# Pooled-query attention and a softplus feed-forward layer: the plan's model of DMAs, its tables, and which pairs' sums TensorE takes

## The chip, the cores and the metric

The kernel runs on one core of a Trainium2 chip. The metric is the device time of one execution in microseconds.

## The reference

```
q_pool = q.reshape(B, H, S // 2, 2, D).mean(axis=3)          # B 4, H 8, S 1152, D 64
scores = scale * np.matmul(q_pool, k.transpose(0, 1, 3, 2))
scores = scores - np.max(scores, axis=-1, keepdims=True)
attn = np.exp(scores)
attn = attn / (np.sum(attn, axis=-1, keepdims=True) + 1e-09)
attn_out = np.matmul(attn, v)
x = attn_out.transpose(0, 2, 1, 3).reshape(B * 576, 512)
h = x @ w_in                                                  # 512 -> 2048
g = np.maximum(h, 0.0) + np.log1p(np.exp(-np.abs(h)))         # softplus
out = g @ w_out                                               # 2048 -> 512
```

Queries are pooled by twos, so there are 576 of them for 1152 keys in each of 32 heads. The two weight matrices arrive as 8-byte floats.

## The kernel before

Two heads make a pair, and there are 16 pairs, numbered 0 to 15; four pairs are a batch. Queries, keys, weights and activations are split into a high and a low f16 part, so that products of f16 keep more digits.

For a pair, `prepare` loads keys, queries and values on SyncE's queue, sums the two queries of a pool (VectorE or GpSimd), finds a scale from squares (ScalarE, a small matmul, a few tiny VectorE steps), writes the high halves (`hi_ways`: ScalarE, GpSimd or VectorE) and the low halves (`lo_ways`: VectorE or GpSimd) and turns keys and queries by DMA transposes (`kT<-kcat`, `qA<-qcat`). `maxima` then computes all scores once, in 27 matmul groups of 384 columns, and VectorE reduces each of them to a negative maximum (`nm<-m`); the maxima become two more columns of the low queries (`qlow<-nm`, the shift steps).

`attention` computes the scores again, turned, in 18 steps for a pair: nine tiles of 128 keys for 256 queries of both heads (512 columns) and nine for 320 (640 columns). In each step TensorE makes the scores (`s`), ScalarE the exponentials (`p`), TensorE the products with the values (`pv`). The sums of the exponentials come in one of two ways. For pairs in `SUMMED` TensorE adds a block of small matmuls with ones to every step (line 871). For the others VectorE or GpSimd adds the tiles `p` elementwise into `acc` (16 adds for a pair), and a closing block of the same size (line 932) sums over the partitions. At the end of a half the sums go out of `rinv` by a small DMA to `few`, get inverted there, go to DRAM (`scratch`) and come back spread over partitions; VectorE or GpSimd multiplies them onto the outputs `xT`.

`feed_forward` takes eight blocks of 256 or 384 rows: matmuls up, softplus on ScalarE, a split into `gh` and `gl`, matmuls down, a store. `weights` decodes `w_in` in eight blocks (1024 KB each, loaded into `gh` and `gl`) and `w_out` in sixteen, mostly on VectorE. `ORDER` interleaves pairs (u) and blocks (U up, D down): pairs 0 to 4 stand alone, then blocks and pairs alternate, and three blocks stand alone at the end.

No order on an engine is written out by hand. Every operation is a `Task` with a priority, the ways (engines) in which it can run, their assumed durations, and the buffers that it takes and gives back. `Sched.run` plays a model of the five queues in time: whenever an engine is free, the ready task with the lowest priority number that fits its buffers is taken, unless another engine would finish it sooner, and is emitted there. So tables and assumed durations decide both the engine and the order. `NUDGE` adds a number to the priority by kind of task and pair or block. VectorE and GpSimd tasks marked "port" are kept apart in that model. On the chip each queue runs in order, and semaphores hold an instruction until what it reads is there.

DMAs all go out on SyncE. Before the change a DMA occupied the model's queue for bytes / 350 + 100 ns (or a fixed number), and its result was `late` by another fixed number.

Of the kernel before, what the change touches and what calls it, by code (L numbers as in the profile page):

```python
# [33 lines left out]
    "up": [-26.25, -7.25, 5.25, -1, 8, -13, -11.5, 6.25],
    "down": [0, -2, 3, -1.75, 12.75, -22.75, -0.25, 7.5],
# [16 lines left out]
class Task:  # L52
    __slots__ = ("ways", "deps", "after", "prio", "take", "give", "ready", "begun", "price", "late")

    def __init__(self, ways, prio, take, give):
        self.ways, self.prio, self.take, self.give = ways, prio, take, give
        self.begun, self.price, self.late = False, {}, 0.0
        self.deps, self.after, self.ready = 0, [], {w[0]: 0.0 for w in ways}


class Sched:
# [9 lines left out]
        "DMA": {"DVE": 100.0, "ACT": 100.0, "POOL": 100.0, "PE": 100.0, "DMA": 1400.0},  # L71
# [22 lines left out]
    def run(self):  # L94
        free = {}
        cold = self.COLD
        port, table = 0.0, "exp"
# [26 lines left out]
        while events:  # L124
# [97 lines left out]
def tile_attention_softplus_ffn(  # L222
# [179 lines left out]
    def load(fn, nbytes, deps, prio, take):  # L402
        return task([("DMA", dma(nbytes), fn)], deps, prio, take=take, late=2600.0)
# [8 lines left out]
    SUMMED = range(5)  # L412
# [84 lines left out]
    def w_in(g, prio):  # L497
# [7 lines left out]
            1 << 19 << (W64 - 1), last_on[g % 2], prio, [])  # L505
# [32 lines left out]
    def w_out(f, prio):  # L538
# [6 lines left out]
        def words(e):  # L545
# [3 lines left out]
                  1 << 18 << (W64 - 1), [], prio, [r])  # L549
# [42 lines left out]
    def prepare(u):  # L592
# [14 lines left out]
        def low():  # L607
# [12 lines left out]
            2 * S * D * 4, [], prio - 6.0, [r])  # L620
# [26 lines left out]
        ql = load(load_q, 1000000, [], prio - 6.0, [qr])  # L647
# [9 lines left out]
        for h in range(2):  # L657
# [496 lines left out]
```

## Time and profile before

| | |
|---|---|
| three runs, us | 863.42, 863.89, 864.05 |
| profiled execution, us | 864.61 |
| its span, us | 862.5 |
| TensorE busy, us (share) | 815.5 (95%) |
| VectorE | 608.2 (71%) |
| ScalarE | 424.1 (49%) |
| GpSimd | 197.9 (23%) |
| granted TensorE clock | 0.998 of 2.4 GHz |

The span is the time from the first to the last instruction in the profiled execution. Busy time is the time in which an engine has an instruction in work; TensorE's matmuls are pipelined, so it can be busy and yet not at its peak. Shares over the whole span mix parts of the program with different limits; the rows below are cut by stretches.

### The profile page before, as it was taken

The page shows a single profiled execution, that of the slowest core. Times are in us where ns is not written, and L with a number is a line of the kernel's source. Part 1 is how long each engine was busy: PE and PEld are TensorE (multiplying, and loading weights), DVE is VectorE, ACT ScalarE, POOL GpSimd, SP SyncE. Part 2 cuts the span into 40 slices and gives each one's busy share as a digit, 9 for nine tenths or more (in the row PEclk, how much of TensorE's full clock was granted, in tenths as well). Part 3 has the DMA queues.
Part 4 walks back from the last instruction along what each step waited for, and adds up shares of the span by engine and source line. Part 5 has one row for each costly group of instructions (what it writes and reads, how often), then busy time and mean ns, then how long its engine had stood idle before and what let it go on. Part 6 is the DMA issues. An engine that isn't in the chain of part 4 may idle for free.

```text
span 862.5 us, 24388 instructions
## 1 busy us (share of the span) xinstructions
PE 815.5 (95%) x10452; PEld 570.8 (66%) x10452; DVE 608.2 (71%) x1260; ACT 424.1 (49%) x688; POOL 197.9 (23%) x187
## 2 busy tenths in 40 slices
PE   1999999999999999999999999999999999999997
PEld 0555555558766696778867676667966778695653
DVE  5989988889999768976795675858785773251520
ACT  3668656787675425464354553437354472120210
POOL 0000101000685223642251311524230400000000
PEclk9999999999999999999999999999999999999999
DMA  9756665767423215246315050242004000000000
GB/s 249 185 157 182 138 158 159 142 198 203 131 64 77 80 37 120 50 117 80 78 41 133 14 146 14 57 110 59 26 28 103 21 17 8 34 2 26 2 14 25
DMA packets 101612, 75.12 MB, mean 87 GB/s; under 512 B 68480, under 2 KB 82816, under 8 KB 101504
## 3 DMA queue, kind: packets, MB, share of 16 engines
q1 hardware_dynamic: 101504, 73.57, 33.9%
q8 instruction: 82, 1.34, 0.7%
q14 instruction: 26, 0.21, 0.1%
HBM read 49.81 MB, written 4.79 MB: 63 GB/s over the span
## 4 chain that ended last, share of the span: by engine, by line
PE 69%; DMA 14%; DVE 12%; ACT 2%; issue 2%; SPq 0%; POOL 0%; ACTq 0%; DVEq 0%
PE s L326 31%; PE m L326 25%; PE pv L864 11%; DVE nm L721 5%; DMA few<-rinv 4%; DMA rinv<-scratch 3%; DMA kT<-kcat 2%; PE pv L871 2%; ACT p L855 1%; DVE kcat L318 1%; DMA scratch<-few 1%; DMA raw<-in_q_dram 1%; DMA qA<-qcat 1%; DVE qlow L318 1%; DMA v<-in_v_dram 1%
## 5 line engine op out<-in xcount | busy, mean ns | idle before, releaser
L855 ACT ACTIVATE p<-s,cols 128x640 f32<-128x640 f32 (+1 forms) x288 | 206.8, 739 | 126.4 <-PE s L326 86.7
L721 DVE TENSOR_REDUCE nm<-m 128x1 f32<-128x384 f32 x432 | 219.0, 547 | 49.4 <-PE m L326 47.1
L864 PE MATMUL pv<-p,v 128*64 128x320 f32 (+1 forms) x1152 | 188.5, 415 | 0.2 <-ACT rinv L940 0.2
L326 PE MATMUL m<-w,gh 128*64 128x512 f16 x1152 | 176.0, 381 | 0.0
L326 PE MATMUL s<-qA,kT 128*64 128x320 f16 (+1 forms) x1152 | 156.0, 287 | 4.3 <-ACT p L855 4.3
L326 PE MATMUL s<-qB,kB 66*64 66x320 f16 (+1 forms) x1152 | 156.5, 287 | 0.0
L398 POOL TENSOR_TENSOR acc<-acc,p 128x512 f32<-128x512 f32 (+1 forms) x82 | 121.3, 1479 | 94.9 <-ACT p L855 63.9
L326 PE MATMUL m<-kT,qA 128*64 128x384 f16 x864 | 119.3, 330 | 19.6 <-DMA kT<-kcat 11.1
L326 PEld LDWEIGHTS <-w1h 128*64 128x64 f16 x2048 | 113.3, 110 | 18.9 <-issue 3.8
L326 PE MATMUL m<-w,gl 128*64 128x512 f16 x576 | 113.0, 381 | 0.0
L1093 ACT ACTIVATE g<-s,blk 128x512 f32<-128x512 f32 (+1 forms) x80 | 51.5, 643 | 124.5 <-PE s L326 115.7
L326 PEld LDWEIGHTS <-gh 128*64 128x64 f16 x1152 | 69.9, 110 | 49.8 <-issue 1.8
L864 PEld LDWEIGHTS pv<-p,v 128*64 128x64 f32 x1152 | 74.1, 136 | 34.5 <-issue 19.2
L326 PEld LDWEIGHTS <-kT 128*64 128x64 f16 x1152 | 75.3, 111 | 24.3 <-issue 8.8
L326 PEld LDWEIGHTS <-qA 128*64 128x64 f16 x864 | 56.3, 110 | 51.5 <-issue 24.9
L326 PE MATMUL s<-xh,w1h 128*64 128x256 f16 (+1 forms) x1024 | 84.5, 286 | 1.3 <-ACT g L1093 1.3
L326 PE MATMUL s<-xl,w1h 128*64 128x256 f16 (+1 forms) x1024 | 84.4, 286 | 0.0
L326 PE MATMUL s<-xh,w1l 128*64 128x256 f16 (+1 forms) x1024 | 84.4, 286 | 0.0
L326 PEld LDWEIGHTS <-kB 66*64 66x64 f16 x1152 | 72.6, 110 | 16.2 <-issue 5.5
L398 DVE TENSOR_TENSOR acc<-acc,p 128x640 f32<-128x640 f32 (+1 forms) x72 | 55.5, 771 | 19.3 <-ACT p L855 12.4
L315 DVE TENSOR_SCALAR gh<-g,blk 128x384 f16<-128x384 f32 (+1 forms) x55 | 25.4, 463 | 59.6 <-ACT g L1093 59.5
L326 PEld LDWEIGHTS <-w1l 128*64 128x64 f16 x1024 | 57.2, 110 | 6.3
(126 smaller groups left out, 777.9 us busy)
## 6 DMA issues: line engine op xcount, KB each, us to landing
raw<-in_k_dram SPq DMA_DIRECT2D x16, 576.0 KB
v<-in_v_dram SPq DMA_DIRECT2D x16, 576.0 KB
raw<-in_q_dram SPq DMA_DIRECT2D x64, 128.0 KB
raw<-in_moe_w_out_dram SPq DMA_DIRECT2D x16, 512.0 KB
kB<-kT SPq DMA_DIRECT2D x32, 144.0 KB
gh<-in_moe_w_in_dram SPq DMA_DIRECT2D x4, 1024.0 KB
gl<-in_moe_w_in_dram SPq DMA_DIRECT2D x4, 1024.0 KB
out_dram<-o SPq DMA_DIRECT2D x16, 256.0 KB
```

The costliest lines, as they stand in the source:

```text
L315: nc.vector.tensor_scalar(out=out_, in0=in_, scalar1=s1, scalar2=s2, op0=op0, **kw)
L318: nc.vector.scalar_tensor_tensor(out=out_, in0=in0, scalar=s, in1=in1, op0=op0, op1=op1)
L326: nc.tensor.matmul(out=out_[c:e], lhsT=lhsT[:, c:e], rhs=rhs, start=start, stop=stop, tile_position=(0, at + c))
L398: e.tensor_tensor(out=o, in0=a, in1=b, op=op)
L721: parts.append(task([("DVE", dve(384), lambda: nc.vector.tensor_reduce(out=x.nm3.item[:, c, g:g + 1], in_=ps.item[:, 0:384], axis=AX.X, op ...
L855: nc.scalar.activation(out=pt.item[:, :, 0:n], in_=s.item[:, :, 0:n], func=ACTF.Exp, scale=x.sc)
L864: nc.tensor.matmul(out=pv.item[h * 64:(h + 1) * 64, 0:n], lhsT=x.v.item[:, h, kt], rhs=pt.item[:, h, 0:n], start=(kt == 0), stop=(kt == KT ...
L871: nc.tensor.matmul(out=pv.item[g:g + 32, 512 - n // 2:512], lhsT=ones[:, 0:32], rhs=pt.item[:, h, a * n // 2:(a + 1) * n // 2], start=Fals ...
L1093: x = task([("ACT", act(N, 1, 1), lambda: nc.scalar.activation(out=gs.item[:, 0:N], in_=ps.item[:, 0, 0:N], func=ACTF.Softplus, scale=ih[: ...
```

## The change

The model of a DMA gets two parts: the time that SyncE's queue needs to issue it, and a wire that all DMAs share in order, on which it lies for a time of its own; it lands 1340 ns after it leaves the wire. The argument `late` goes. `SUMMED` shrinks from pairs 0 to 4 to pairs 0, 2 and 4, so pairs 1 and 3 get adds and a closing block instead of sums in every step. A new table `LEAN` adds a price by engine (GpSimd, ScalarE), kind of task and pair or block to tasks that can run on several engines. All numbers of `NUDGE` are new. The arithmetic is otherwise the same; SyncE issues as many DMAs as before.

```diff
-    "most": [2.75, -1.75, -5.5, 2.25, 0.75, 6, -0.75, 1.75, -35.25, -21, 0, 3.75, -0.75, -1.25, -4, 7],
...
+    "most": [6.75, -0.75, 4.5, 2.75, 0, -7, 4, -0.25, -10.25, -38.5, 4.75, -24.25, 1, 1.25, -5.25, 0],
...
+LEAN = {
+    "POOL": {
+        "prep": [-200, 0, 2400, 300, -300, -800, -650, 750, 100, -1200, -600, -350, -50, -1050, 350, -600],
...
+        t.price = {e: LEAN[e][kind][i] for e in LEAN if len(ways) > 1}
...
-    GIVE = {"DMA": 2000.0, "PE": 200.0}
+    GIVE = {"DMA": 100.0, "PE": 200.0}
...
+    LANDS = 1340.0
...
+                    if e == "DMA":
+                        if w[4:]:
+                            free[e] = max(done, wire + w[4])
+                            wire = free[e] + tag
+                        else:
+                            wire = max(max(now + 390.0, wire) + tag, done + 75.0)
+                        done = wire + self.LANDS
...
-                            u.ready[x] = max(u.ready[x], done + t.late + self.LAG[e].get(x, 150.0))
+                            u.ready[x] = max(u.ready[x], done + self.LAG[e].get(x, 150.0))
...
-    def load(fn, nbytes, deps, prio, take):
-        return task([("DMA", dma(nbytes), fn)], deps, prio, take=take, late=2600.0)
+    def load(fn, queue, wire, deps, prio, take):
+        return task([("DMA", queue, fn, wire)], deps, prio, take=take)
...
-    SUMMED = range(5)
+    SUMMED = (0, 2, 4)
...
-            1 << 19 << (W64 - 1), last_on[g % 2], prio, [])
+            390.0, 2000. * W64, last_on[g % 2], prio, [])
...
-        x.k_done = task([("DMA", 2500.0, lambda: nc.sync.dma_start_transpose(
-            out=x.kT.item, in_=cat.item.rearrange("p t d -> p (t d)")))], parts, prio, take=[x.kT], give=[cat],
-            late=2600.0)
+        x.k_done = task([("DMA", 2000.0, lambda: nc.sync.dma_start_transpose(
+            out=x.kT.item, in_=cat.item.rearrange("p t d -> p (t d)")), 1150., 1700.0)], parts, prio,
+            take=[x.kT], give=[cat])
...
-                    sums.price = {"DVE": 500.0}
+                    sums.price["DVE"] = 500.0
```

Two places of the new order matter below. The first is the start of the program. On SyncE's queue, after the loads of pair 0 (`raw_72` its keys, `raw_73` its queries), the loads of pair 1 (`raw_74`, `raw_75`), the values `v` of pairs 0 and 1, blocks of `w_in` (into `gh`, `gl`) and the two transposes of pair 0 stand so before:

```order
L697 DMA v_76<-in_v_dram 128x2x576
L617 DMA raw_74<-in_k_dram 128x2x576
L640 DMA raw_75<-in_q_dram 128x256 x2
L644 DMA raw_75<-in_q_dram 64x128
L640 DMA raw_75<-in_q_dram 128x256 x2
L644 DMA raw_75<-in_q_dram 64x128
L697 DMA v_77<-in_v_dram 128x2x576
L684 DMA_TRANSPOSE qA_86<-qcat_83 128x9x128
L670 DMA_TRANSPOSE kT_79<-kcat_78 128x18x128
L502 DMA gh<-in_moe_w_in_dram 128x4x512
L617 DMA raw_73<-in_k_dram 128x2x576
L677 DMA kB_81<-kT_79 64x1152 x2
```

and so in the changed kernel:

```order
L651 DMA raw_74<-in_k_dram 128x2x576
L674 DMA raw_75<-in_q_dram 128x256 x2
L678 DMA raw_75<-in_q_dram 64x128
L674 DMA raw_75<-in_q_dram 128x256 x2
L678 DMA raw_75<-in_q_dram 64x128
L731 DMA v_76<-in_v_dram 128x2x576
L536 DMA gl<-in_moe_w_in_dram 128x4x512
L731 DMA v_77<-in_v_dram 128x2x576
L536 DMA gh<-in_moe_w_in_dram 128x4x512
L718 DMA_TRANSPOSE qA_86<-qcat_83 128x9x128
L704 DMA_TRANSPOSE kT_79<-kcat_78 128x18x128
L651 DMA raw_73<-in_k_dram 128x2x576
```

Two blocks of `w_in` now stand ahead of the transposes, and the keys of pair 1 ahead of the values of pair 0.

On VectorE, behind the last sum of queries (`raw_75`), the first reductions of maxima (`nm<-m`) of pair 0 come at once before:

```order
L398 TENSOR_TENSOR raw_75<-raw_75 128x9x64
L692 COPY qA_86<-qA_86 128x64
L721 TENSOR_REDUCE nm_0_123<-m_109 128x1
L721 TENSOR_REDUCE nm_0_123<-m_110 128x1
L721 TENSOR_REDUCE nm_0_123<-m_108 128x1
```

In the changed kernel the decode of a block of `w_in` (`raw<-raw`, `raw<-gl`, its scale in `tw`, `invw` and `sw`, its low half `w1l`) stands ahead of them:

```order
L432 TENSOR_TENSOR raw_75<-raw_75 128x9x64
L349 TENSOR_SCALAR raw_72<-raw_72 128x1024
L352 SCALAR_TENSOR_TENSOR raw_72<-gl,raw_72 128x1024 x2
L349 TENSOR_SCALAR tw<-m_109 128x1
L349 TENSOR_SCALAR tw<-tw 128x1
L349 TENSOR_SCALAR invw<-tw 128x1
L377 RECIPROCAL sw<-invw 128x1
L352 SCALAR_TENSOR_TENSOR w1l<-raw_72,sw,w1h 128x4x256
L755 TENSOR_REDUCE nm_0_123<-m_110 128x1
L755 TENSOR_REDUCE nm_0_123<-m_108 128x1
```

Four passes over 1024 columns and four tiny steps have moved ahead of the first maximum.

The second place is pair 1 on GpSimd. Before, between the high halves of keys (`kcat`) that it writes for pairs 0 to 2 there are small copies alone (`qA`), and then products with the reciprocals (`xm`, `xT`):

```order
L369 TENSOR_SCALAR kcat_78<-raw_72,cols 128x9x64
L369 TENSOR_SCALAR kcat_78<-raw_74,cols 128x9x64
L691 COPY qA_87<-qA_87 128x64
L369 TENSOR_SCALAR kcat_78<-raw_73,cols 128x9x64
L691 COPY qA_86<-qA_86 128x64
L398 TENSOR_TENSOR xm_68<-xm_68,rinv_97 128x64
L398 TENSOR_TENSOR xT_66<-xT_66,rinv_97 128x256
L369 TENSOR_SCALAR kcat_78<-raw_72,cols 128x9x64
```

In the changed kernel the adds of pair 1 stand there:

```order
L403 TENSOR_SCALAR kcat_78<-raw_74,cols 128x9x64
L725 COPY qA_87<-qA_87 128x64
L432 TENSOR_TENSOR acc_94<-p_91,p_93 128x2x256
L432 TENSOR_TENSOR acc_94<-acc_94,p_90 128x2x256
L432 TENSOR_TENSOR acc_94<-acc_94,p_91 128x2x256
L432 TENSOR_TENSOR acc_94<-acc_94,p_93 128x2x256
L432 TENSOR_TENSOR xT_66<-xT_66,rinv_96 128x256
L432 TENSOR_TENSOR acc_94<-acc_94,p_90 128x2x256
L432 TENSOR_TENSOR acc_94<-acc_94,p_92 128x2x256
L432 TENSOR_TENSOR acc_95<-p_93,p_90 128x640
L432 TENSOR_TENSOR acc_95<-acc_95,p_92 128x640
```

GpSimd has taken 13 of the 16 adds of pair 1, and a product with a reciprocal stands among them; the adds of pair 3 follow in the same manner.

## Rows read from the trace of the kernel before

**Rows 1.** Busy us (and instructions) of each engine by stretch, clock, DMA share, GB/s

```profile
61.00:95.90 34.90, 34.35 (x472) 19.87 (x469) 32.20 (x79) 24.19 (x40) 4.90 (x5) 1.00 0.55 150
...
61.00:224.00 163.00, 153.72 (x2176) 97.96 (x2172) 144.76 (x336) 116.62 (x205) 16.23 (x23) 1.00 0.68 169
...
223.80:324.20 100.40, 96.48 (x1240) 72.64 (x1240) 82.29 (x148) 52.30 (x84) 51.82 (x39) 0.98 0.25 68
324.20:709.00 384.80, 376.60 (x4708) 274.33 (x4705) 286.19 (x595) 193.43 (x306) 124.49 (x109) 1.00 0.29 68
709.00:862.50 153.50, 148.14 (x1852) 102.90 (x1848) 45.90 (x88) 29.22 (x45) 2.66 (x5) 1.00 0.05 16
```

The first columns are the stretch and its length; then follow PE, PEld, DVE, ACT and POOL.

**Rows 2.** VectorE by form, 20 to 200 us: count, busy, mean ns, idle before

```profile
L721 DVE TENSOR_REDUCE nm<-m 128x1 f32<-128x384 f32 x152 | 77.7, 546 | 4.0 <-PE m L326 3.7
L318 DVE SCALAR_TENSOR_TENSOR w<-raw,w 128x512 int32<-128x512 int32 x18 | 12.0, 678 | 0.0
L318 DVE SCALAR_TENSOR_TENSOR w1l<-raw,sw,w1h 128x1024 f16<-128x1024 f32 x8 | 10.2, 1277 | 0.2 <-ACT w1h L365 0.2
...
L318 DVE SCALAR_TENSOR_TENSOR kcat<-raw,cols,kcat 128x576 f16<-128x576 f32 x10 | 7.8, 815 | 0.0
L315 DVE TENSOR_SCALAR qcat<-raw,cols 128x1152 f16<-128x1152 f32 x5 | 7.0, 1401 | 0.0
...
L398 DVE TENSOR_TENSOR raw<-raw 128x576 f32<-128x576 f32 x5 | 3.7, 746 | 0.7 <-DMA raw<-in_q_dram 0.7
...
L398 DVE TENSOR_TENSOR xT<-xT,rinv 128x256 f32<-128x256 f32 x6 | 2.5, 421 | 3.7 <-DMA rinv<-scratch 3.7
...
L318 DVE SCALAR_TENSOR_TENSOR qlow<-nm,qlow 128x5 f16<-128x5 f32 x5 | 0.9, 173 | 0.0
...
L950 DVE RECIPROCAL few<-few 128x5 f32<-128x5 f32 x4 | 0.7, 186 | 3.0 <-DMA few<-rinv 3.0
```

**Rows 3.** Timeline of TensorE, 17 to 20 us: start, us, instruction, idle before

```profile
18.69 1.71 PE L326 MATMUL m<-kT,qA 128*64 128x384 f16 x8 [9.81 <-DMA kT<-kcat]
```

**Rows 4.** Timeline of SyncE's queue at the start, issues alone

```profile
9.12 0.59 SPq L697 DMA_DIRECT2D v<-in_v_dram  x1
11.25 1.37 SPq L684 DMA_TRANSPOSE qA<-qcat  x1
```

**Rows 5.** Busy time by stretch, as rows 1, 2 to 13 us

```profile
2.00:13.00 11.00, 0.38 (x4) 0.29 (x4) 8.26 (x12) 3.14 (x7) 0.75 (x1) 1.00 0.99 313
```

**Rows 6.** Timeline of TensorE in pair 0, second half

```profile
48.18 0.48 PE L871 MATMUL pv<-p,ones 128*32 128x160 f32 x8
48.59 0.76 PE L864 MATMUL pv<-p,v 128*64 128x320 f32 x4
```

**Rows 7.** GpSimd by form, 224 to 324 us

```profile
L398 POOL TENSOR_TENSOR acc<-acc,p 128x512 f32<-128x512 f32 x14 | 20.6, 1473 | 3.4 <-ACT p L855 2.7
L398 POOL TENSOR_TENSOR acc<-acc,p 128x640 f32<-128x640 f32 x10 | 17.1, 1710 | 6.6 <-ACT p L855 5.0 <-DVE acc L398 1.2
```

**Rows 8.** VectorE by form, 224 to 324 us

```profile
L318 DVE SCALAR_TENSOR_TENSOR w<-w,m 128x512 f16<-128x512 f32 x15 | 15.0, 1002 | 1.4 <-ACT w L365 1.2
...
L315 DVE TENSOR_SCALAR w<-w,m 128x512 f16<-128x512 f32 x5 | 4.5, 900 | 0.1
...
L318 DVE SCALAR_TENSOR_TENSOR kcat<-raw,cols,kcat 128x576 f16<-128x576 f32 x2 | 2.5, 1316 | 0.0
L398 DVE TENSOR_TENSOR raw<-raw 128x576 f32<-128x576 f32 x2 | 2.4, 1210 | 0.0
L318 DVE SCALAR_TENSOR_TENSOR qlow<-nm,qlow 128x5 f16<-128x5 f32 x2 | 2.2, 1109 | 0.0
```

**Rows 9.** Timeline of VectorE, two weight splits with no GpSimd instruction beside them

```profile
263.70 0.49 DVE L315 TENSOR_SCALAR w<-w,m 128x512 f16<-128x512 f32 x1
264.22 0.75 DVE L318 SCALAR_TENSOR_TENSOR w<-w,m 128x512 f16<-128x512 f32 x1
```

More of the change, by code (lines that the diff above doesn't have):

```diff
@@ L34 @@
-    "up": [-26.25, -7.25, 5.25, -1, 8, -13, -11.5, 6.25],
-    "down": [0, -2, 3, -1.75, 12.75, -22.75, -0.25, 7.5],
+    "prep": [7.25, 3.25, 3, 4, 2.5, -11.5, 12.75, 3.75, -2.25, 3, 0, 13.75, 29.25, 23, -0.75, 3.5],
+    "value": [0, 0, 1.25, -7, 0, -18.75, -2.25, 7.75, 0, -5.75, 0, 12.5, 16.5, 7.5, 0, -72.75],
+    "most": [6.75, -0.75, 4.5, 2.75, 0, -7, 4, -0.25, -10.25, -38.5, 4.75, -24.25, 1, 1.25, -5.25, 0],
+    "shift": [-27.75, 0.75, 3, -1, 4.75, 9, 1.25, 0, 17.5, 0, 7.25, 1, 4, 15.25, -1.5, 8.75],
@@ L52 @@
 class Task:
-    __slots__ = ("ways", "deps", "after", "prio", "take", "give", "ready", "begun", "price", "late")
+    __slots__ = ("ways", "deps", "after", "prio", "take", "give", "ready", "begun", "price")
     def __init__(self, ways, prio, take, give):
         self.ways, self.prio, self.take, self.give = ways, prio, take, give
-        self.begun, self.price, self.late = False, {}, 0.0
+        self.begun, self.price = False, {}
         self.deps, self.after, self.ready = 0, [], {w[0]: 0.0 for w in ways}
@@ L70 @@
         "POOL": {"DVE": 50.0, "ACT": 60.0, "POOL": 50.0, "PE": 60.0, "DMA": 1300.0},
-        "DMA": {"DVE": 100.0, "ACT": 100.0, "POOL": 100.0, "PE": 100.0, "DMA": 1400.0},
+        "DMA": {"DVE": 100.0, "ACT": 100.0, "POOL": 100.0, "PE": 100.0, "DMA": 150.0},
     }
-    GIVE = {"DMA": 2000.0, "PE": 200.0}
+    GIVE = {"DMA": 100.0, "PE": 200.0}
     OVER = {"DVE": 80.0, "ACT": 105.0}
@@ L81, in __init__, with task @@
         self.label = None
-    def task(self, ways, deps=(), prio=0.0, take=(), give=(), late=0.0):
+    def task(self, ways, deps=(), prio=0.0, take=(), give=()):
         kind, i = self.label
         t = Task(ways, prio + NUDGE[kind][i], list(take), list(give))
-        t.late = late
+        t.price = {e: LEAN[e][kind][i] for e in LEAN if len(ways) > 1}
         for d in deps:
@@ L96, in run @@
         cold = self.COLD
-        port, table = 0.0, "exp"
+        port, wire, table = 0.0, 0.0, "exp"
         for t in self.tasks:
@@ L645, in load_q @@
                                   in_=q[b, 2 * p + h, 1024:1152].rearrange("(i r) d -> i (r d)", r=2))
-        ql = load(load_q, 1000000, [], prio - 6.0, [qr])
+        ql = load(load_q, 3100.0, 2600., [], prio - 6.0, [qr])
         y = task(tt_ways(576, lambda: (qs(), qs(), raw()[:, :, 1]), ALU.add), [ql], prio)
@@ L677, in high_keys @@
                 nc.sync.dma_start(out=x.kB.item[0:D, ks], in_=x.kT.item[h * D:(h + 1) * D, ks])
-        x.kB_done = task([("DMA", 1100.0, high_keys)], [x.k_done], prio + 4.0, take=[x.kB], late=2400.0)
+        x.kB_done = task([("DMA", 1170.0, high_keys, 1600.)], [x.k_done], prio + 4.0, take=[x.kB])
         prio += 1.0
@@ L683, in prepare @@
                          [y], prio, take=[x.qlow], give=[qr])
-        x.q_done = task([("DMA", 1400.0, lambda: nc.sync.dma_start_transpose(
-            out=x.qA.item[:, 0:T], in_=qc.item.rearrange("p t a d -> p (t a d)")))], [y], prio, take=[x.qA],
-            give=[qc, qr], late=1900.0)
+        x.q_done = task([("DMA", 1350.0, lambda: nc.sync.dma_start_transpose(
+            out=x.qA.item[:, 0:T], in_=qc.item.rearrange("p t a d -> p (t a d)")), 640.0, -500.0)], [y], prio,
+            take=[x.qA], give=[qc, qr])
         def beside(e):
@@ L1067, in store @@
                         nc.sync.dma_start(out=dst, in_=o.item[first - t * 128:first - t * 128 + m])
-            task([("DMA", dma(1 << 18), store)], [x], when[4 * t + 3] + 1.0, give=[o])
+            task([("DMA", 350.0, store, 440.0)], [x], when[4 * t + 3] + 1.0, give=[o])
         g_free = new_g
```

75 lines of the change are left out of this document (50 added, 25 removed).

## Prediction

> **What bounds the kernel now.** I read the stretches between the first exponentials of certain pairs first, then the waits of each engine inside them. Pairs are numbered 0 to 15. In pairs 1 to 4 (61.0 to 224 us) VectorE is busy 144.76 of 163 us [rows 1]; TensorE stands in that view with 153.72, but a busy TensorE includes matmuls that lie in its pipeline, and GpSimd has only 16.23. In the same part the reduction of the maxima, VectorE's largest form, idles only 3.7 us for TensorE [rows 2]. So VectorE sets the pace there. From pair 5 on it turns round: TensorE is busy 96.48 of 100.4 us and then 376.6 of 384.8, VectorE 82.29 and 286.19; in the last 153.5 us the other engines have little left [rows 1]. What is to be had behind 223.8 us is therefore the 12.1 us in which TensorE is not busy; ahead of it, what VectorE is spared. The beginning has a limit of its own: TensorE stands 9.81 us until the transposed keys of pair 0 have landed, and its first matmul of maxima starts at 18.69 us [rows 3].
>
> **The sum**, made against the profiled execution (864.61 us: a span of 862.5 and 2.1 around it; the median of the three runs is 863.89, 0.7 lower).
>
> *Start.* In the new order of SyncE's queue two more loads stand ahead of the two transposes of pair 0: two weight blocks of 1024 KB. Before, the last load ahead of them is issued at 9.12 us and the query transpose at 11.25 [rows 4], while the wire moves 313 GB/s at a DMA share of 0.99 [rows 5]. The wire is full, so 2.1 MB more are 2.1 MB / 313 GB/s = 6.7 us for the transposes, if they queue behind the loads. The first maxima then start at about 25.4. VectorE uses the gap for the decode of one weight block, which is new ahead of the first maximum: four passes over 1024 columns, none longer than the 1.277 us of the last one [rows 2], and four tiny steps. Four of 1.277 are 5.1 us, which fit into 6.7 and are costed at nothing (without that cover 5.1 us). Between the first maximum and pair 1's first scores VectorE now has 8 more reductions (0.546 us) and 2 more low halves of keys (0.815 us) [rows 2], 6.0 us; it is about nine tenths busy there, and some of this meets its idle time: +5.4. Start: **+12.1 us**. Bounds: +5.4 if the transposes do not wait for the loads, +17.2 if the decode isn't covered.
>
> *Pairs 1 to 4, VectorE.* By the two orders VectorE loses there 5 query copies (1.401 us, now on ScalarE), 4 low halves of keys (0.815), 4 decode steps (0.678) and 3 query sums (0.746; two go to GpSimd) [rows 2]: 7.0 + 3.3 + 2.7 + 2.2 = 15.2 us. Smaller ones (products with the reciprocals, high halves) and three adds that it gains cancel roughly. Some of this is the work that the start now does. Four fifths of the loss lie in pair 1. There TensorE becomes the next limit: it is busy 34.35 of 34.9 us [rows 1], and the change takes away its 18 blocks of sums at up to 0.41 us (from the start of the block to the start of the products) [rows 6], 7.4 us. So pair 1 can shrink by 34.9 - 27.0 = 7.9 us, not by the 12 us of VectorE. The remaining fifth, 3 us, and 1 us for a preparation that moves behind pair 5 come off pairs 2 to 4: **-11.9 us**. Bounds: -15.2 if only VectorE counts, -7.9 if only pair 1 gains.
>
> *Sums on TensorE.* Pairs 1 and 3 lose 36 such blocks, at most 14.8 us, and get four closing sums of the same size, 1.6 us. As VectorE paces this part, the 13.1 us are not 13.1 us of span. Beyond pair 1 they are worth at most the 3.7 us in which the reductions wait for TensorE [rows 2]: **-2 us** (bounds 0 and -3.7).
>
> *Adds on GpSimd.* Pairs 1 and 3 get 32 adds, of which 29 stand on GpSimd, at 1.47 us and 1.71 us for the two widths [rows 7]. With two query sums, four products and seven high halves of activations moved as well, GpSimd has 50 us more ahead of pair 5. The price is not its own time, but what VectorE loses beside it. The trace has the same situation at pairs 5 and 6: GpSimd is busy 51.82 us [rows 1], and forms of VectorE that read two SBUF operands or write scaled copies are longer than earlier: 2 low halves of keys 1.316 for 0.815, 2 query sums 1.210 for 0.746, 2 of the small shift steps 1.109 for 0.173 [rows 2, 8], and 15 + 5 weight splits 1.002 and 0.900 for 0.75 and 0.49 alone [rows 8, 9]. That is 1.0 + 0.9 + 1.9 + 3.8 + 2.1 = 9.7 us, 0.19 us per us of GpSimd. The reductions stay at 0.546. In pair 1, where TensorE will limit, some 20 of the 50 us are covered; the other 30 cost **+5.7 us**. Bounds: 0 (all in VectorE's idle tenth) and 29 x 0.94 = 27 us (each add holds it once by the longest excess).
>
> The Trainium skill, in SBUF — State Buffer, section "Who interferes with whom", says that VectorE and GpSimd share one pair of ports and that whoever comes first keeps it for the whole instruction, with reductions exempt on this chip. By that rule alone 29 adds could each block a VectorE instruction for nearly their whole 1.47 us or more, over 43 us; the rows agree in kind (the shift step, and the reductions untouched) and show a fifth in size.
>
> *Transfers.* VectorE waits 3.0 us for the small reciprocal transfers and 3.7 us for their broadcast back [rows 2]. The plan now counts a queue and a wire, so that it places these reads later or the transfers earlier. I take **-3 us** of 6.7 (bounds -6.7 and +6.7, as a plan can also place them worse).
>
> *Behind pair 5.* VectorE loses some 22 us by its rows (ten low halves of the activations and twelve products go to GpSimd), GpSimd gains 53. Only TensorE's 12.1 idle us can come back; I take **-5 us**. Bounds: -10, and +10 if GpSimd holds VectorE for 53 x 0.19. The last 153.5 us do not change.
>
> Sum: 12.1 - 11.9 - 2 + 5.7 - 3 - 5 = -4.1 us. 864.6 - 4.1 = 860.5, less 0.7 for the median: **859.8 us**.
>
> **Rivals.**
> *TensorE's saving counts and the adds are free* (0.17). For it: TensorE's busy share is high in pairs 1 to 4 too, and GpSimd's 16.23 us there leave room. Against it: VectorE's own 144.76. The adds' 5.7 us fall away and the sums are worth 3.7: -4.1 - 5.7 - 1.7 = -11.5, or 852 us.
> *The adds on GpSimd hold VectorE* (0.29, slower). A step of VectorE behind an add waits for its end, and the maxima queued behind that step wait too, and TensorE for their buffers. If an add of pairs 1 and 3 costs 0.5 us on the mean (between the 0.25 of the weight splits and the 0.94 of the shift step), it is 14.5 instead of 5.7, and behind pair 5 the same takes 4 of the 5 us gained: -4.1 + 8.8 + 4 = +8.7, or 873 us. It decides from (5.7 + 4.1) / 29 = 0.34 us an add. Against it: in the new order many adds stand beside reductions, which the trace shows untouched. The rule of the Trainium skill named above belongs to this rival.
> *Nothing is left* (0.14). The late start is just made up by pair 1, and the transfers and the stretch behind pair 5 stay as they are: -4.1 + 3 + 1 to 3, or 863 to 866 us.
>
> **How the numbers follow.** The forecast, 855 to 862 us, has 0.40. 0.2% (1.7 us) is about what a measurement of this kernel tells from no change. Faster is the forecast and the first rival, 0.57; same 0.14; slower 0.29. The range takes in the first rival with some room and most of the slower one: 848 to 872 us. The forecast's own range is 855 to 862.
>
> **What would show it.** The first matmul of maxima at 25 to 26 us instead of 18.7; the first exponential of pair 1 at 71 to 75 instead of 61.0, that of pair 2 within 5 us of its old 95.9, that of pair 5 within 4 us of 223.8. VectorE's busy time falls by 15 to 30 us, GpSimd's rises to about 300. The low halves of keys ahead of 224 us are longer than 0.815 us on the mean, but under 1.1. If the transposes land by 20 us, the start's term is wrong; if pair 1 still takes over 33 us, GpSimd's adds limit it; if pair 5 begins later than 230, the second rival holds. The forecast would be wrong as a whole if TensorE's idle time behind pair 5, 12.1 us now, grew instead of shrinking.

## The result, and the profile after

The kernel became slower: 873.64 us (median of four executions, 869.79 to 877.78) against 863.65 for the kernel before (four, 862.84 to 864.05), a ratio of 1.0118 with a 95% interval of 1.007 to 1.0165. Six more executions beside a later run gave 871.73 to 873.75; the median over all ten is 873.4, the yardstick below. In the runs below one execution of f2 (1390.59 us, at a granted clock of 0.567) and one of the kernel before (949.89, at 0.853) were slow ones and are left out. The profiled execution took 874.15 us, 9.5 more than that of before.

The stretches from one first exponential to another, and the tail, in the columns of [rows 1]:

```profile
13.00:40.10 27.10, 11.92 (x76) 5.14 (x78) 21.36 (x46) 13.09 (x20) 1.23 (x3) 1.00 0.97 258
40.10:55.60 15.50, 15.50 (x227) 9.83 (x224) 15.06 (x34) 7.99 (x15) 0.00 (x0) 1.00 0.21 65
55.60:70.50 14.90, 14.90 (x214) 9.05 (x214) 13.02 (x31) 12.20 (x20) 0.00 (x0) 1.00 0.42 126
70.50:98.80 28.30, 26.19 (x318) 19.03 (x318) 26.89 (x48) 19.25 (x31) 21.96 (x14) 1.00 0.56 147
98.80:226.60 127.80, 119.76 (x1628) 81.05 (x1626) 116.39 (x261) 94.00 (x160) 47.94 (x42) 0.97 0.61 147
...
334.90:719.70 384.80, 377.23 (x4718) 275.20 (x4715) 271.20 (x562) 186.12 (x292) 166.82 (x147) 1.00 0.27 63
719.70:872.10 152.40, 147.53 (x1843) 102.37 (x1838) 39.66 (x75) 31.08 (x54) 5.56 (x8) 0.99 0.05 16
226.60:334.90 108.30, 96.90 (x1193) 71.12 (x1191) 90.16 (x160) 59.42 (x99) 56.87 (x45) 0.97 0.49 113
```

Pair 1 now starts at 70.5 us instead of 61.0 and takes 28.3 instead of 34.9; pair 5 starts at 226.6, only 2.8 late. Then pairs 5 and 6 take 108.3 us instead of 100.4 [rows 1], and the rest to the end of the span 537.2 (872.1 - 334.9) instead of 538.3 (862.5 - 324.2). So the span's 9.6 us are 2.8 ahead of pair 5, 7.9 in pairs 5 and 6, and 1.1 given back behind them. TensorE, idle 3.9 us in pairs 5 and 6 before, is idle 11.4 there now. In a second profiled execution of the changed kernel (h2 below, 872.60 us) the same split is 3.6, 4.6 and nothing: the place is the same, the size moves by some 3 us from one execution to the next.

Busy time by engine, from the page:

```profile
PE 810.3 (93%) x10196; PEld 573.1 (66%) x10196; DVE 602.0 (69%) x1223; ACT 427.3 (49%) x689; POOL 302.0 (35%) x266
```

GpSimd has 104 us more. VectorE lost 37 instructions but only 6 us.

What TensorE waits for in pairs 5 and 6 (us in total, times, longest), in the kernel before and in the changed one:

```profile
PE m L326 <- DVE nm L721: 0.3, 1, 0.3
```

```profile
PE m L360 <- DVE nm L755: 7.1, 8, 2.0
PE s L360 <- ACT p L889: 2.2, 4, 0.7
```

TensorE's maxima need one of three PSUM buffers, which VectorE frees by reducing it (`nm<-m`). Before, that wait was 0.3 us; now it is 7.1, nearly the whole loss of the stretch (5.4 in the second profiled execution). The reductions themselves are as quick as ever; forms of VectorE in pairs 5 and 6 of the changed kernel:

```profile
L755 DVE TENSOR_REDUCE nm<-m 128x1 f32<-128x384 f32 x60 | 30.3, 546 | 8.0 <-PE m L360 8.0
...
L432 DVE TENSOR_TENSOR raw<-raw 128x576 f32<-128x576 f32 x2 | 3.5, 1752 | 0.1
...
L352 DVE SCALAR_TENSOR_TENSOR qlow<-nm,qlow 128x4 f16<-128x4 f32 x2 | 2.7, 1372 | 0.0
...
L349 DVE TENSOR_SCALAR cols<-cols 128x2 int32<-128x2 int32 x2 | 2.1, 1073 | 0.0
```

What is long is what stands between them: a query sum of 1.752 us (0.746 undisturbed [rows 2]), shift steps of 1.372 (0.173), tiny steps of the scales of 1.073. VectorE's timeline in the second half of pair 5 shows them in place:

```profile
240.64 1.50 DVE L432 TENSOR_TENSOR raw<-raw 128x576 f32<-128x576 f32 x1
242.06 1.01 DVE L755 TENSOR_REDUCE nm<-m 128x1 f32<-128x384 f32 x2
...
244.29 0.97 DVE L349 TENSOR_SCALAR qlow<-nm 128x4 f16<-128x4 f32 x1
245.17 0.55 DVE L755 TENSOR_REDUCE nm<-m 128x1 f32<-128x384 f32 x1
245.63 1.24 DVE L352 SCALAR_TENSOR_TENSOR qlow<-nm,qlow 128x4 f16<-128x4 f32 x1
...
247.18 1.50 DVE L349 TENSOR_SCALAR cols<-cols 128x2 int32<-128x2 int32 x1
```

The adds of pair 5 run on GpSimd at the same time; three of them:

```profile
243.62 1.61 POOL L432 TENSOR_TENSOR acc<-acc,p 128x640 f32<-128x640 f32 x1
245.31 1.53 POOL L432 TENSOR_TENSOR acc<-acc,p 128x640 f32<-128x640 f32 x1
246.92 1.74 POOL L432 TENSOR_TENSOR acc<-acc,p 128x640 f32<-128x640 f32 x1
```

They end at 245.23, 246.84 and 248.66 us (start plus duration). The steps that VectorE starts at 244.29, 245.63 and 247.18 end at 245.26, 246.87 and 248.68, each 0.02 to 0.03 us behind an add: a short step lasts as long as what is left of the add beside it; below, the add holds it. The preparation of pair 7 (`raw`, `cols`) stands here in the new plan; before, it stood behind 256 us, among splits of weights, and TensorE's waits for VectorE in pairs 5 and 6 came to 1.9 us in all.

### The profile page after: what moved, and what is told of

Its sections match the earlier page's. It is cut to its first block, busy times and chain, and to the rows that moved or that the text cites. A ratio compares the mean times of both kernels' runs of the same rounds, so it can differ in the third digit from the quotient of the medians.

```text
span 872.1 us, 23968 instructions
## 1 busy us (share of the span) xinstructions
PE 810.3 (93%) x10196; PEld 573.1 (66%) x10196; DVE 602.0 (69%) x1223; ACT 427.3 (49%) x689; POOL 302.0 (35%) x266
## 4 chain that ended last, share of the span: by engine, by line
PE 71%; DVE 13%; DMA 8%; ACT 4%; issue 2%; POOL 1%; SPq 1%; DVEq 0%; ACTq 0%; POOLq 0%
PE s L360 30%; PE m L360 26%; PE pv L898 12%; DVE nm L755 6%; DMA qA<-qcat 3%; DMA v<-in_v_dram 2%; PE pv L905 1%; ACT p L889 1%; ACT raw L520 1%; DMA raw<-in_moe_w_out_dram 1%; DVE w L352 1%; DMA raw<-in_q_dram 1%; DVE raw L432 1%; DMA kT<-kcat 1%; DVE qlow L352 1%
## 5 line engine op out<-in xcount | busy, mean ns | idle before, releaser
L889 ACT ACTIVATE p<-s,cols 128x512 f32<-128x512 f32 (+1 forms) x288 | 208.2, 740 | 146.1 <-PE s L360 70.0
L432 POOL TENSOR_TENSOR acc<-acc,p 128x640 f32<-128x640 f32 (+1 forms) x112 | 167.9, 1501 | 58.7 <-ACT p L889 38.7
L360 PE MATMUL s<-qA,kT 128*64 128x256 f16 (+1 forms) x1152 | 159.3, 290 | 7.7 <-ACT p L889 7.3
L360 PE MATMUL s<-qB,kB 66*64 66x256 f16 (+1 forms) x1152 | 159.8, 290 | 0.0
L360 PE MATMUL m<-kT,qA 128*64 128x384 f16 x864 | 126.2, 338 | 17.9 <-DVE nm L755 11.8
L360 PEld LDWEIGHTS <-kT 128*64 128x64 f16 x1152 | 79.0, 112 | 35.5 <-issue 17.4
L898 PEld LDWEIGHTS pv<-p,v 128*64 128x64 f32 x1152 | 80.5, 138 | 29.7 <-issue 12.7
L403 POOL TENSOR_SCALAR gh<-g,blk 128x512 f16<-128x512 f32 (+1 forms) x33 | 26.5, 804 | 144.8 <-ACT g L1127 120.5
L352 DVE SCALAR_TENSOR_TENSOR gl<-g,blk,gh 128x512 f16<-128x512 f32 (+1 forms) x71 | 50.7, 714 | 30.6 <-POOL gh L403 27.9
L432 DVE TENSOR_TENSOR acc<-acc,p 128x640 f32<-128x640 f32 (+1 forms) x70 | 58.6, 837 | 10.1 <-ACT p L889 8.3
```

The source lines that it names most:

```text
L352: nc.vector.scalar_tensor_tensor(out=out_, in0=in0, scalar=s, in1=in1, op0=op0, op1=op1)
L360: nc.tensor.matmul(out=out_[c:e], lhsT=lhsT[:, c:e], rhs=rhs, start=start, stop=stop, tile_position=(0, at + c))
L403: nc.gpsimd.tensor_scalar(out=o, in0=i, scalar1=s, scalar2=0.0, op0=ALU.mult, op1=ALU.add)
L432: e.tensor_tensor(out=o, in0=a, in1=b, op=op)
L889: nc.scalar.activation(out=pt.item[:, :, 0:n], in_=s.item[:, :, 0:n], func=ACTF.Exp, scale=x.sc)
L898: nc.tensor.matmul(out=pv.item[h * 64:(h + 1) * 64, 0:n], lhsT=x.v.item[:, h, kt], rhs=pt.item[:, h, 0:n], start=(kt == 0), stop=(kt == KT ...
```

## Experiments

My theory was that the loss arises in pairs 5 and 6 because VectorE got more work there (a preparation and decodes of `w_out`) and transposes late in SyncE's queue. The rivals: the GpSimd adds hold VectorE, in pairs 1 and 3 or in 5 and 6; the half-speed stretches of TensorE's clock, of which the changed kernel has more; and the late start.

The kernel before was timed beside each of them, with medians of 862.3 to 863.2 us. Stretches are from one profiled execution each, cut at first exponentials; as the two of the changed kernel differ by 3.3 us in pairs 5 and 6, smaller differences there say little:

```
                              pair 5 begins   pairs 5 and 6   median, us
before                            223.8          100.4        862.3 to 863.7
changed                           226.6          108.3        873.4
changed, again                    227.4          105.0
e1 no adds in pairs 1, 3          222.1          106.7        869.92
e2 no adds in pairs 5, 6          228.2           96.4        862.98
e3 before, no adds in 5, 6        222.9           94.6        857.01
e4 transposes of pair 7 first     227.2          108.5        874.56
e5 less decode in pairs 5, 6      227.4          104.1        874.02
e6 before, more VectorE work      222.7          112.3        872.99
e7 before, more work, no adds     221.5          103.6        866.26
e8 start put right                229.2          103.7        872.16
f1 gaps of TensorE filled         226.4          109.3        876.62
f2 adds in two pieces             228.3          100.6        867.00
f3 before, adds in two pieces     223.4           99.0        859.65
g1 gaps filled, half as much      228.3          105.0        871.46
g2 before, adds in four pieces    223.4          103.1        870.71
h1 f2, g1 and e8 together         223.6          103.9        867.86
```

**The adds left out.** e1 and e2 are the changed kernel, e3 the kernel before. The GpSimd adds of the named pairs are left out but for the first of each half, so their sums miss keys; the order of everything else is kept.

```diff
+                    ways = tt_ways(2 * n, add, ALU.add)
+                    if x.u in (5, 6) and kt > 1:      # e1: (1, 3)
+                        ways[0] = ways[0][:2] + (lambda: None,) + ways[0][3:]
```

> The changed kernel without the GpSimd adds of pairs 1 and 3, except the first add of each half (25 of 29 are left out, so the sums of these two pairs miss keys); TensorE's and VectorE's own work is as it was. If the adds hold VectorE on the path, pair 5 begins 8 to 13 us earlier than at 226.6 us and the end comes as much earlier. If the loss arises behind pair 5, in pair 6, pair 5 begins at most 4 us earlier and the end moves by no more than that.

> The changed kernel without the GpSimd adds of pairs 5 and 6, except the first add of each half (the sums of these pairs miss keys). If the adds hold VectorE in pairs 5 and 6, pair 6 shrinks from 81.9 us by more than 6 us, to about the 73.4 us of before. If the late transposes and VectorE's moved preparation make the loss, it shrinks by at most 3 us.

> The kernel before without the GpSimd adds of pairs 5 and 6, except the first add of each half: the yardstick for the same edit on the changed kernel. If the adds cost the changed kernel more than they cost the kernel before, this run gains 2 to 3 us where the other gains over 6; if they cost both alike or nothing, both gain the same within 2 us.

Measured: e1 869.92 us, 3.5 less than the changed kernel, or 0.14 us for each of the 25 adds. e2 862.98, 10.4 less, and pairs 5 and 6 shrink to 96.4 us. e3 857.01, 5.8 less than before. If the gains of e1 and e2 add up, which no run tested, the adds cost the changed kernel 13.9 us and the kernel before 5.8, and the difference of 8.1 us is most of the loss of 10. GpSimd does no more adds in pairs 5 and 6 than before (25 against 28, of which 22 and 24 were left out), but they cost nearly twice as much.

They do not hold VectorE longer, though. First pairs 5 and 6 in e3 and e2, then pairs 1 to 4 in the changed kernel and in e1, in the columns of [rows 1]:

```profile
222.90:317.50 94.60, 93.91 (x1237) 71.95 (x1232) 69.74 (x148) 51.95 (x85) 12.83 (x15) 1.00 0.26 72
```

```profile
228.20:324.60 96.40, 91.79 (x1194) 67.52 (x1192) 77.36 (x160) 58.80 (x99) 24.32 (x23) 1.00 0.51 128
```

```profile
70.50:226.60 156.10, 145.94 (x1944) 100.08 (x1944) 143.28 (x308) 113.26 (x190) 69.90 (x55) 0.98 0.60 147
```

```profile
70.50:222.10 151.60, 144.57 (x1944) 100.12 (x1945) 132.56 (x308) 112.81 (x190) 28.23 (x30) 0.98 0.62 151
```

Without the adds the same number of VectorE's instructions takes 12.6 us less in the kernel before (69.74 for 82.29), 12.8 less in the changed one (77.36 for 90.16), and 10.7 less in its pairs 1 to 4 (132.56 for 143.28). The kernels gain 5.8, 10.4 and 3.5 us by it. So nearly the same hold costs very different amounts, by its place. An add also frees a `p` buffer for ScalarE when it ends, but that is not what the runs gain: ScalarE's wait for the adds in pairs 5 and 6 falls from 2.8 to 1.2 us in e2 and from 1.2 to nothing in e3, and in f2 below it rises to 4.8 while the kernel gains.

**Transposes late in SyncE's queue.** I had seen VectorE wait 3.2 us at 263 us for the transposed queries of pair 7, which two loads delayed.

```diff
-        kl = load(lambda: nc.sync.dma_start(
+        kl = load(lambda: held.append(load_k) if u == 8 else load_k(),
...
+            if u == 7:
+                for issue in held:
+                    issue()
```

> The changed kernel with the k load of pair 8 and the v load of pair 7 issued on SyncE behind both transposes of pair 7 instead of ahead of them; nothing else moves. If the transposes that stand late in the queue make pair 6 long, pair 6 and the end come 3 to 6 us earlier. If the GpSimd adds or the work on VectorE alone do it, they move by less than 1 us.

Measured: 874.56 us, and pairs 5 and 6 at 108.5. VectorE's wait for these queries is gone from the profile and no time is gained, so that half of my theory fell.

**VectorE's work in pairs 5 and 6**, taken away from the changed kernel (e5), added to the kernel before (e6), added there without the adds (e7).

```diff
+            elif k in (2, 3) and not whole:            # e5: w_out 2, 10, 12, 14, 15
+                pass
...
+                for _ in range(times):                 # e6, e7: 3 for w_out 9 and 12
                     stt(ti, lo, 29, ti, ALU.logical_shift_right, ALU.bitwise_or)
```

> The changed kernel without two of the three VectorE passes in the decodes of five blocks of w_out (2, 10, 12, 14 and 15), those that lie in pairs 5 and 6: 10 instructions of 0.68 us, 6.8 us of VectorE, about as much as the change moved into this stretch. These blocks lose signs and low bits, so the output differs. If VectorE has no slack left in pairs 5 and 6, so that every hold by a GpSimd add comes through, the stretch shrinks from 108.3 us by 4 to 7 us and the end with it. If the adds cost more only because of where they lie against ScalarE and the p buffers, it shrinks by at most 2 us.

> The kernel before with 7.0 us more work on VectorE in pairs 5 and 6, all of it repeated passes that change nothing: the two OR passes of two w_out blocks three times instead of once (8 x 0.68 us) and the two low halves of keys of pair 7 twice (2 x 0.81 us). If VectorE's slack there is what absorbed the adds before, the stretch of pairs 5 and 6 grows from 100.4 us by 4 to 7 us and the end comes as much later (about 868 to 870 us). If the amount of work on VectorE there is not what counts, it grows by at most 2 us.

> The same 7.0 us more work on VectorE in the kernel before, and no GpSimd adds in pairs 5 and 6 except the first of each half (the sums of these pairs miss keys). Against the run without adds and without the work (857.0 us). If adds and work share one slack, this work costs at most 3 us here, clearly less than with the adds. If the work costs by itself, whatever the adds do, it costs the same 4 to 7 us as with them.

Measured: e5 874.02 us, no gain at all (its profiled execution, 870.98, is its fastest); e6 872.99, 9.8 more than before; e7 9.2 more than e3. So VectorE's work is not one slack that it shares with the adds, and the other half of my theory fell as well. About the same amount of work (6.8 and 7.0 us) is worth nothing at one place and more than its own length at another, with adds or without. In e6 the decode passes that run three times stand among the reductions for pair 6 (two low halves of keys that run twice come later); nearly the whole loss lies in pair 5 (first columns as in [rows 1]), where TensorE is busy 28.23 of 37.6 us (27.0 us long in the kernel before), at a granted clock of 0.91, which may have a part in the loss:

```profile
222.70:260.30 37.60, 28.23 (x314) 20.14 (x314) 33.84 (x64) 18.17 (x31) 20.65 (x15) 0.91 0.18 53
```

In the changed kernel six of the ten decode passes that e5 leaves out stand ahead of 235.8 us, where the first reductions of the stretch come; the other four have reductions close behind them. So the amount of work on VectorE alone is not the cause. That what counts is what stands ahead of a reduction whose buffer TensorE needs would fit e2, e3 and e6, but no run moved the same work from one place to the other.

**The start.** Both transposes of pair 0 go ahead of the two `w_in` blocks, and the first decode goes behind the first maxima; done by moving entries in the finished plan. On SyncE's queue:

```diff
+DMA v_77<-in_v_dram
+DMA_TRANSPOSE qA_86<-qcat_83
+DMA_TRANSPOSE kT_79<-kcat_78
 DMA gl<-in_moe_w_in_dram
-DMA v_77<-in_v_dram
 DMA gh<-in_moe_w_in_dram
-DMA_TRANSPOSE qA_86<-qcat_83
-DMA_TRANSPOSE kT_79<-kcat_78
```

> The changed kernel with the start put right by hand: both transposes of pair 0 ahead of the first two blocks of w_in on SyncE's queue, and the decode of the first block behind the maxima of pair 0 on VectorE. Nothing is left out; behind 60 us the order is as it was. If the late start costs its whole 9.5 us, the first exponential comes 8 to 11 us earlier than at 40.1 us and the end 6 to 10 us earlier. If pair 1 and VectorE's work only move the loss, the first exponential comes earlier by as much, but pair 2 and the end by at most 4 us.

Measured: 872.16 us; the gain of 1.2 lies within the spread of the executions. The first exponential comes at 34.6 us, 5.5 earlier, but pair 1 begins at 70.6 as before (70.5):

```profile
13.00:34.60 21.60, 10.66 (x62) 4.25 (x63) 17.63 (x37) 9.08 (x14) 1.23 (x3) 0.99 0.98 247
34.60:55.80 21.20, 19.25 (x236) 12.29 (x237) 19.08 (x43) 11.76 (x20) 0.00 (x0) 0.85 0.41 129
55.80:70.60 14.80, 14.80 (x214) 8.97 (x212) 12.99 (x31) 12.12 (x19) 0.00 (x0) 1.00 0.40 120
```

VectorE is busy 49.7 us between 13 and 70.6, against 49.4 in the changed kernel between 13 and 70.5. So the late transposes alone do not make the start. What does is open: VectorE has the same work ahead of pair 1, but TensorE, busy 30.4 of the 30.4 us from 40.1 to 70.5 in the changed kernel, is busy 34.05 of 36.0 here, and ran at a granted clock of 0.85 in the first 21.2 of them.

**The clock.** In the profile of the changed kernel the granted clock falls to half speed (1.2 GHz) in five stretches, 17 us in all, each time after TensorE had stood, and only once in that of before (the fall at the very end of both not counted). Here, in steps of 1 us:

```profile
268.00:269.00 1.00, 0.01 (x1) 0.00 (x0) 1.00 (x3) 0.67 (x3) 1.00 (x2) 1.00 0.85 215
269.00:270.00 1.00, 0.79 (x6) 0.44 (x6) 1.00 (x3) 0.00 (x0) 0.92 (x2) 1.00 0.61 164
270.00:271.00 1.00, 0.22 (x1) 0.00 (x0) 1.00 (x3) 0.00 (x0) 1.00 (x1) 1.00 0.99 214
...
273.00:274.00 1.00, 1.00 (x14) 0.31 (x12) 0.84 (x2) 0.64 (x1) 0.00 (x0) 0.60 0.77 280
274.00:275.00 1.00, 1.00 (x10) 0.65 (x12) 0.90 (x2) 0.16 (x1) 0.00 (x0) 0.50 0.16 51
```

f1 and g1 put idle matmuls at nine such places, f1 208 of them, g1 half.

```diff
+        for _ in range(n):
+            nc.tensor.matmul(out=pv_only[0:64, 320:352], lhsT=ones[:, 0:64], rhs=ones[:, 0:32], ...
```

> The changed kernel with idle matmuls (64 x 32, into unused columns of the accumulator of the products, 208 in all) put into TensorE's queue at nine places where TensorE stood for 0.6 to 3.5 us in the profile, most of them just ahead of a half-speed stretch. Nothing is left out and no other engine has a changed order. If the half-speed clock behind such gaps costs time of its own, the mean granted clock rises from 0.989 to 0.994 or more and the kernel becomes 3 to 5 us faster. If the low clock only accompanies waits that cost the time anyway, the clock rises and the time stays within 1.5 us.

> The idle matmuls of the run before in half the number (they lasted twice as long as meant: 34 records took 2.12 us), so that none outlasts the gap that it fills. If the half-speed clock costs time of its own, the clock stays at 0.994 or more and the kernel is now 3 to 5 us faster than the changed one (869 to 871). If the clock falls in time that is lost anyway, it stays at 872 to 875.

Measured: f1 876.62 us at a clock of 0.999. No half-speed stretch is left but the one at the end, yet it is slower: the matmuls lasted twice as long as meant (2.12 us at 268.50, for a gap of 1.14), so f1 doesn't judge the theory. g1 does, in part: 871.46 us, clock 0.995 to 0.999, with two of the five stretches left in its profile and none of them in pairs 5 and 6. Its ratio to before, 1.0074 to 1.0106, still overlaps that of the changed kernel. So this puts the clock at about 2 us of the 10, less than the 3 to 5 that the theory wanted. That most low-clock time lies where TensorE would have waited for VectorE anyway would explain it, but is not shown. Among the ten executions of the changed kernel the fastest (869.79) had the highest mean clock (0.996) and the slowest (877.78) the lowest (0.986); which of the two leads to the other is not shown either.

**The length of a hold.** Each add on GpSimd becomes two, one for each head (f2 changed, f3 before), or four (g2).

```diff
+            if halves and e is nc.gpsimd:
+                for h in range(2):
+                    e.tensor_tensor(out=o[:, h], in0=a[:, h], in1=b[:, h], op=op)
+                return
```

> The changed kernel with each add on GpSimd issued as two adds of one head each, so that GpSimd works 10 to 15% longer in all but each of its instructions is about half as long. If a step of VectorE is held until the GpSimd add beside it ends, the holds become half as long: the change gains 3 to 6 us and VectorE's excess falls by a third or more. If the adds cost time through their sum (ScalarE waiting for p buffers, or the total of GpSimd's work), it gets slower by 1 to 4 us.

> The same two adds for one in the kernel before. If the length of one hold counts, it becomes 2 to 3 us faster (half of the 5.8 us that the adds of pairs 5 and 6 cost). If the sum of GpSimd's work counts, it is the same or up to 3 us slower.

> The kernel before with each add on GpSimd issued as four pieces. If the length of one hold decides, another 1 to 2 us come off the 859.7 us of the two pieces; if GpSimd's own length (up by some 40%) or its late p buffers weigh by then, it is 1 to 4 us slower than with two pieces.

Measured: f2 867.0 us (median of four), 6.4 less than the changed kernel. f3 859.65, a ratio of 0.9966 to before (0.9953 to 0.9979): 2.6 us faster than the kernel before and the fastest of all that compute everything. g2 870.71, 7.7 slower than before. The adds of pairs 5 and 6 in f2, on GpSimd by form:

```profile
L434 POOL TENSOR_TENSOR acc<-acc,p 128x320 f32<-128x320 f32 x26 | 24.8, 982 | 0.0
L434 POOL TENSOR_TENSOR acc<-acc,p 128x256 f32<-128x256 f32 x18 | 14.0, 808 | 5.1 <-DVE few L988 4.2 <-ACT p L893 0.8
```

and in the changed kernel:

```profile
L432 POOL TENSOR_TENSOR acc<-acc,p 128x640 f32<-128x640 f32 x13 | 21.0, 1614 | 0.6
L432 POOL TENSOR_TENSOR acc<-acc,p 128x512 f32<-128x512 f32 x9 | 12.2, 1355 | 5.4 <-DVE few L984 4.2 <-ACT p L889 0.8
```

One instruction falls from 1.614 to 0.982 us and from 1.355 to 0.808, while the sum rises from 33.2 to 38.8. TensorE's wait for the reductions and VectorE's steps at the same place in f2:

```profile
PE m L360 <- DVE nm L759: 2.8, 4, 1.1
```

```profile
242.36 1.00 DVE L436 TENSOR_TENSOR raw<-raw 128x576 f32<-128x576 f32 x1
...
245.66 0.30 DVE L349 TENSOR_SCALAR qlow<-nm 128x4 f16<-128x4 f32 x1
245.86 0.54 DVE L759 TENSOR_REDUCE nm<-m 128x1 f32<-128x384 f32 x1
246.33 0.45 DVE L352 SCALAR_TENSOR_TENSOR qlow<-nm,qlow 128x4 f16<-128x4 f32 x1
...
247.77 0.82 DVE L349 TENSOR_SCALAR cols<-cols 128x2 int32<-128x2 int32 x1
```

The four steps that took 5.2 us take 2.6, and the wait goes from 7.1 to 2.8. Not every step gains: a pass over a weight block between them (`w<-w`) goes from 0.41 to 1.09, so that the way from the start of the query sum to the next reduction behind `cols` shrinks from 8.0 to 6.1 us. Over pairs 5 and 6 VectorE's 160 instructions take 85.34 us instead of 90.16, so 4.8 of the 12.8 us of hold come back.

With four pieces the holds shrink again (VectorE is busy 74.06 us in pairs 5 and 6 of g2, 79.89 in f3, 82.29 in the kernel before), but the adds now end later, and ScalarE waits for the `p` buffers that they free; in f3 and in g2 over the whole program:

```profile
ACT p L859 <- POOL acc L400: 4.0, 5, 2.3
```

```profile
ACT p L860 <- POOL acc L401: 14.3, 15, 2.9
```

**Parts of the change.** Here the plan was made anew, so the whole order moves.

```diff
-    SUMMED = range(5)                                  # f4, in the kernel before
+    SUMMED = (0, 2, 4)
...
-        t.price = {e: LEAN[e][kind][i] for e in LEAN if len(ways) > 1}    # g4, in the changed kernel
```

g3 is the changed kernel with the old `NUDGE`, no `LEAN` and the old `SUMMED`, so that the model of DMAs alone is new.

> The kernel before with one part of the change alone: TensorE sums pairs 0, 2 and 4 instead of 0 to 4, with the old tables and the old model of DMAs, and the plan made anew. If the sums on TensorE were a burden in pairs 1 and 3, it is 2 to 6 us faster; if the adds on GpSimd hold VectorE, 2 to 8 us slower; if the tables fit only the plan that they were made for, more than 8 us slower whatever the sums do.

> One part alone: the new model of DMAs in the kernel before, with its old table of priorities, no prices and TensorE's sums for pairs 0 to 4; the plan is made anew. If the model makes better plans by itself, it is 1 to 5 us faster than before; if the tables fit only the plan for which they were made, it is more than 8 us slower.

> One part undone: the changed kernel without the table of engines' prices, the rest of the change kept; the plan is made anew. If the prices send work to GpSimd that VectorE would better have kept, it is faster than the changed kernel (873.6 us); if the tables fit only the plan for which they were made, it is more than 8 us slower.

Measured: 907.65, 870.30 and 894.60 us. The choice of sums alone costs 45 us with tables made for another plan, the prices alone are worth 21. The model of DMAs alone costs 7. None of the parts can be said to carry the loss: each table fits one plan, and a part exchanged alone gives a new plan that nothing was fitted to.

**Together.** h1 has the edits of f2, g1 and e8; h2 is the changed kernel once more.

> The changed kernel with three of the repairs at once: the GpSimd adds in two pieces (6.2 us by itself), the gaps of TensorE filled with half the idle matmuls (2.2 us) and the start put right (1.5 us). Nothing is left out. If the three losses lie in different places and add up, it comes to 863 to 865 us, level with the kernel before. If they share one wait (the maxima on VectorE in pairs 5 and 6), it stays at 866 to 868 us.

> The changed kernel as it is, on the same chip and in the same rounds as the run before, since its four executions so far ranged from 869.8 to 877.8 us. 872 to 875 us; a median below 871 us would shrink the gains told of the other runs by as much.

Measured: h1 867.86 us (863.83 to 875.83), h2 873.16. f2, g1 and e8 gained 6.4, 1.9 and 1.2 alone and 5.5 together: they don't add up, and beside f2 the other two bring nothing. That the clock and the start are other faces of the one wait for VectorE would fit this, but is not shown.

## Why the prediction was wrong

**The step that failed** is *Behind pair 5* (-5 us, with the sentence that only TensorE's 12.1 idle us could come back). Pairs 5 and 6, the rest and the tail came to +6.8 in the profiled execution (+4.5 in the second one). I read from 96.48 of 100.4 that TensorE is the bound there, and took GpSimd's adds there for paid. e3 shows that they cost 5.8 us already before, and e6 that VectorE had no room among the reductions: TensorE was the bound because each reduction came just in time. The new plan put a preparation with its tiny steps among the reductions beside running adds; VectorE, which was to lose 22 us behind pair 5, gained 7.9 in pairs 5 and 6 (90.16 for 82.29). I had entered that preparation as 1 us off pairs 2 to 4 and at nothing where it arrived. My upper bound for this step (+10, if GpSimd holds VectorE for 0.19 us per us) had the mechanism and was the nearer end to the truth, but by luck: it priced the 53 us that GpSimd gains, and 42 of them came behind pair 6 (166.82 for 124.49 [rows 1]), where the time did not grow. The sign named for an error as a whole, TensorE's idle time behind pair 5 growing from 12.1 us, came true: 11.4 + 7.6 = 19.0 up to the last exponential.

**Adds on GpSimd ahead of pair 5** (+5.7): e1 measures 3.5. Right in kind, too high, though the hold was sized too low: 9.7 us by rows 8 in pairs 5 and 6, where e3 measures 12.6; 0.14 us an add is far from the 0.34 at which the rival was to decide. Low halves of keys there, named as a sign at 0.815 to 1.1 us, were 0.994 on the mean.

**The slower rival** gave the time (873) and the mechanism, a step of VectorE held by an add with the maxima queued behind it, but put most of it in pairs 1 and 3. It decided in pairs 5 and 6, where the adds were not new. Its time is partly luck: 14.5 us for the adds of pairs 1 and 3, where e1 measures 3.5, made up for what it left out behind them. The third rival's sum does not follow from its words: with the transfers and pair 5 as before it is -4.1 + 3 + 5, or 868 us.

**Start** (+12.1): pair 1 began 9.5 us late. The first maxima start at 23.73 us, near the 25.4 forecast, but the 6.7 us for the transfers are not what made it late: in e8 the first exponential comes 5.5 us earlier and pair 1 no earlier. Which part did is open, as said there.

**Pairs 1 to 4** (-11.9 and -2): pair 1 shrank by 6.6 of the 7.9 us foreseen, and pairs 2 to 4 by 0.1 in all, adds included (-0.3 by my terms). **Transfers** (-3): VectorE's waits for the reciprocals fell from 6.7 to 1.6 us ahead of 200 us, as hoped. Taken together the terms ahead of pair 5 came to +0.9, and pair 5 began 2.8 late, within the 4 that were allowed.

**VectorE's busy time** was to fall by 15 to 30 us and fell by 6. The adds of pairs 1 and 3, which are new, hold it for 10.7 us by e1; without that hold the fall lies in the range.

The Trainium skill, SBUF — State Buffer, section "Who interferes with whom", says that VectorE and GpSimd share a pair of ports and that whoever issues first keeps it for its whole instruction. The trace agrees: three steps end 0.02 to 0.03 us behind the adds beside them, with adds of half the length the four steps above shrink by half, and the reductions stay at 0.546 and 0.547 us. Which of the steps of the new plan brings how much of the wait beyond that was not separated; moving the preparation alone was not tried.

## What to carry to other kernels

Where a queue interleaves tiny steps with the work that another engine waits for, price a hold where it lies, not by its mean: 24 GpSimd adds that hold VectorE for 12.6 us cost 5.8 us of time in one plan, 22 that hold it for 12.8 cost 10.4 in another, and 25 that hold it for 10.7 cost 3.5 elsewhere. An engine that is 96% busy need not be the bound of a stretch; look who frees its buffers, and how late. If long instructions of GpSimd stand beside such a queue, cut them in two before anything is planned anew, and stop when the consumer of their results begins to wait.

## What the runs showed of the hardware

An add of 512 columns on GpSimd costs 1.36 to 1.47 us, and one of 256 costs 0.81: cutting is cheap down to that size, and at 128 columns (0.51 us) the sum is half as much again. TensorE's granted clock went to half speed after TensorE had stood, in five stretches, 17 us in all; idle matmuls in the gaps brought its mean to 0.999 in f1, which was 3.2 us slower, and to 0.995 to 0.999 in g1, which was 1.9 us faster. With two loads of 1024 KB ahead of it, SyncE spent 4.99 us on the issue of a transpose that took 1.37 before [rows 4], and 1.37 again in e8, where these loads stand behind it; the second transpose took 4.70 us for 3.89 before:

```profile
11.81 4.99 SPq L718 DMA_TRANSPOSE qA<-qcat  x1
16.92 4.70 SPq L704 DMA_TRANSPOSE kT<-kcat  x1
```
